# Where the moving operands of a fused attention and two-layer MLP kernel start, modulo 128 bytes

## The chip, the cores and the metric

One core of a Trainium2 chip. The metric is the device time of one execution in microseconds (us), median of the runs; lower is better.

## The reference, cut to what matters

Windowed attention over 4 x 8 heads of 576 positions (head size 64), then two dense layers without bias over 2304 tokens, 512 wide with 2048 hidden units: `relu(h)^2` in the first, `h * cos(h)` in the second. Everything is float32.

```python
def _attn_ref(q, k, v):                       # (4, 8, 576, 64)
    scores = np.matmul(q, k.transpose(0, 1, 3, 2)) / np.sqrt(D)
    rel = pos[:, None] - pos[None, :]
    scores = np.where((rel >= 0) & (rel < 64), scores, -1e9)
    attn = softmax(scores)
    return np.matmul(attn, v)

def reference(**kwargs):
    x = attn_out.transpose(0, 2, 1, 3).reshape(2304, 512)
    h = np.maximum(x @ moe_w_in, 0.0)         # 512 -> 2048
    x = h * h @ moe_w_out                     # 2048 -> 512
    h = x @ moe2_w_in
    return (h * np.cos(h)) @ moe2_w_out
```

## The kernel before

**Products in two words.** A float32 number is held as two words of the type float32r, hi and lo, and each 128x128 block of a product is three matmuls: hi x hi, hi x lo, lo x hi. A matmul reads two operands from the on-chip memory (SBUF): the stationary one, 128 columns, which a weight load puts into TensorE beforehand, and the moving one, 256, 384 or 512 columns that stream past it. A column is 4 bytes in each partition. The weight load for the next matmul runs while the present one streams.

**Stages.** (1) Attention for the first tokens, while the weights of layer 1 are converted. (2) Layer 1 for tokens 0 to 1279 in units (class `UnitA`, and `Half` for the first unit's first four hidden blocks, split in two): `g1` (L1803) multiplies a weight tile `W_in_w...` by the tokens in the tile `X` into `ph`; ScalarE and VectorE make `relu^2` and its hi and lo words in `g`; `g2` (L1129, L1196) multiplies `W` by `g` into `accA`. `g1` of a unit's hidden block runs two blocks ahead of its `g2`, so the two alternate, 12 matmuls each. The attention of later tokens is strewn in. (3) Layer 1 for the last 1024 tokens by Strassen's seven products (`group1`, L1642): the pieces B11, B21, T3 and T4 are in `X`, T1 in a tile `x_more`, T2 and B22 in tiles of their own (`piece`). Its second half is `job1` (L1720, `accC`). (4) Layer 2 in three passes of 768 tokens (`group`, L1514, outputs `x`, `y`, `z`): the 14 pieces of 384 columns lie in `X` and four of them in `x_more` (function `piece`). Its second half is `Job.tile_op` (L1472, `accB`), where the activations `gb_e`, `gb_a`, `gb_b` are stationary and the weights `wo` move.

**What sets the order.** A planner (class `Plan`) orders all operations by keys, due times and modelled costs, and writes them out; the engines then run their queues in order. No address enters the planner.

**Addresses.** Tiles of the pool `cp` stand one after the other at the start of SBUF, and the pools with the weights and activations follow. `X` is laid out as `[P, 2, 2, 4, 512]`. Units 0 and 3 and units 5 and 6 start at column 0 of its halves; unit 2 (256 columns) starts at column 8 of the second (`x_col`). Layer 2's pieces start `SIDE` = 8 columns behind the start of a half. The tiles `g` are 512 columns, read from column 8 where the unit is 256 wide.

Of the kernel before, what the change touches and what calls it, by code (L numbers as in the profile page):

```python
# [9 lines left out]
F32 = mybir.dt.float32  # L10
# [6 lines left out]
P = 128  # L17
# [11 lines left out]
def f32(ap):  # L29
    return ap.bitcast(F32)  # L30
# [212 lines left out]
def kernel(  # L243
# [26 lines left out]
    UA = 256  # L270
    H = 384
    TW = 2 * H
    H1 = 512
# [6 lines left out]
    SIDE = 8  # L280

    psum = bass.MemoryType.PSUM
    cp = ctx.enter_context(tc.tile_pool(name="cp", bufs=1))
# [20 lines left out]
    pair = cp.tile([P, 8], F32, name="hpi")  # L304
    hpi, spare = pair[:, 0:1], pair[:, 4:5]
    quarter = cp.tile([P, 1], F32, name="quarter")
    X = cp.tile([P, 2, 2, NCC, 2 * UA], F32R, name="X")
    still = cp.tile([P, 2, P], F32, name="still")
    nc.vector.memset(still[:, 0], 0.0)
    nc.vector.memset(still[:, 1], 1.0)  # L310
# [14 lines left out]
    def copy(e, o, i, scale=1.0):  # L325
        if e == "ACT":
            nc.scalar.activation(o, i, AF.Copy, scale=scale)  # L327
        elif e == "POOL":
            nc.gpsimd.tensor_scalar(o, i, scale, 1.0, ALU.mult, ALU.mult)
        elif scale == 1.0:  # L330
            nc.vector.tensor_copy(o, i)
        else:
            nc.vector.tensor_scalar(o, i, scale, None, ALU.mult)
# [333 lines left out]


    spans = [(0, 2), (2, 1), (3, 2)]
    x_col = [0, UA, 2 * UA + 8, 0, UA, 2 * UA, 3 * UA]  # L670
    x_before = [
        [m for m in range(n) if abs(x_col[m] - x_col[n]) < UA][-1:] for n in range(len(x_col))]
    xr = R["W"].buf()
# [4 lines left out]
    def packed(n, g, key, sp, k_s=None):  # L678
# [65 lines left out]
        def gather(eng, e):  # L744
# [8 lines left out]
            for i in range(HB):  # L753
# [7 lines left out]
            nc.vector.tensor_reduce(  # L761
                t["mm"][:, e], S[:, :, :, 0:WINDOW], mybir.AxisListType.X, ALU.max, negate=True)

# [98 lines left out]
        def sl(i):  # L862
            return slice(off + i * P, off + i * P + P)

        def hi(eng):
            for i in range(HB):
                copy(eng, X[:, half, 0, cs, sl(i)], t["O"][i])

        def lo(eng):
            for i in range(HB):  # L870
                nc.vector.tensor_tensor(  # L871
                    X[:, half, 1, cs, sl(i)], t["O"][i], f32(X[:, half, 0, cs, sl(i)]), ALU.subtract)

# [8 lines left out]
    def attention(n, g, key, sp, k_s=None):  # L882
# [162 lines left out]
        def hi(eng):  # L1045
            copy(eng, X[:, half, 0, cs, sl], t["O"])

        def lo(eng):
            nc.vector.tensor_tensor(
                X[:, half, 1, cs, sl], t["O"], f32(X[:, half, 0, cs, sl]), ALU.subtract)  # L1050

# [8 lines left out]
    bp = {}  # L1060
# [4 lines left out]
    class UnitA:  # L1065
# [10 lines left out]
        def x(self, hl, c):  # L1076
            return X[:, self.half, hl, c, self.sl]

# [193 lines left out]
    def piece1(o, c, hl):  # L1272
        if o in (B11, B21):
            return X[:, 1, hl, c + 2 * (o == B21)]
        if o in (T3, T4):
            v = X[:, 0].rearrange("p l c n -> p (l c n)")[:, 4 * H1 * (o == T4):][:, 0:4 * H1]
        elif o == T1:
            v = bp["x"][:, SIDE:SIDE + 4 * H1]
        else:
            v = whole1[o].tile  # L1280
        return v[:, (2 * c + hl) * H1:(2 * c + hl + 1) * H1]

    def prepare1(key, free):
# [12 lines left out]
        def whole(o, c):  # L1296
            return f32(piece1(o, c, 0)), f32(piece1(o, c, 1))
# [17 lines left out]
        def split(o, c, src, deps, bufs):  # L1315
            dst = [whole1[o]] if o in whole1 else []

            def hi(e):
                if dst and dst[0].tile is None:
                    dst[0].tile = wp.tile([P, 8 * P * 2], F32R, tag=f"W{dst[0].slot}", name=f"piece_{o}")  # L1320
                copy(e, piece1(o, c, 0), src())

            def lo(e):
                tt(piece1(o, c, 1), src(), f32(piece1(o, c, 0)), ALU.subtract)

            take, used = use(*dst, *bufs)
            h = op({"ACT": act_us(H1), "DVE": dve_us(H1, True)}, key, hi,
                   [*deps, *free.get(o, ())], take, used)
            l = op({"DVE": dve_us(H1)}, key, lo, [h], use=[*dst, *bufs])
            ready1[o, c] = [h, l]  # L1330
            return [h, l]
# [771 lines left out]
```

## Time and profile before

| | |
|---|---|
| median of 3 runs | 837.73 us (836.99 to 841.36) |
| the profiled execution's own time | 836.86 us |
| its span, first to last instruction | 835.1 us |
| matmuls (PE) busy | 827.4 us, 99% of the span |
| weight loads (PEld) busy | 723.8 us |
| VectorE (DVE), ScalarE (ACT) busy | 657.3 us, 470.9 us |

PE is TensorE's matmul side, PEld its weight loads, which run beside matmuls. Matmuls are pipelined: one begins streaming before the one before it has left the array, so that the recorded length of a matmul is more than the distance to the next one's start. This distance is what a matmul costs in a dense stream. It is read from the timeline, where the start of a row less that of the row before it, divided by the number of matmuls in the row before, gives it; rows are given to 0.01 us.

### The profile page before, as it was taken

The page shows a single profiled execution, that of the slowest core. Times are in us where ns is not written, and L with a number is a line of the kernel's source. Part 1 is how long each engine was busy: PE and PEld are TensorE (multiplying, and loading weights), DVE is VectorE, ACT ScalarE, POOL GpSimd, SP SyncE. Part 2 cuts the span into 40 slices and gives each one's busy share as a digit, 9 for nine tenths or more (in the row PEclk, how much of TensorE's full clock was granted, in tenths as well). Part 3 has the DMA queues.
Part 4 walks back from the last instruction along what each step waited for, and adds up shares of the span by engine and source line. Part 5 has one row for each costly group of instructions (what it writes and reads, how often), then busy time and mean ns, then how long its engine had stood idle before and what let it go on. Part 6 is the DMA issues. An engine that isn't in the chain of part 4 may idle for free.

```text
span 835.1 us, 14747 instructions
## 1 busy us (share of the span) xinstructions
PE 827.4 (99%) x5628; PEld 723.8 (87%) x5628; DVE 657.3 (79%) x1325; ACT 470.9 (56%) x1044; POOL 14.4 (2%) x40
## 2 busy tenths in 40 slices
PE   8999999999999999999999999999999999999997
PEld 8898889997787888888888999988999988999986
DVE  6998869889697886776879788885788885788851
ACT  7999546665355743444531656563556653656642
POOL 2300000000000000000000000000000000000000
PEclk9999999999999999999999999999999999999999
DMA  9884157868587749988999693062643062742011
GB/s 346 326 331 139 56 174 277 302 208 312 193 285 273 284 170 370 326 300 312 355 411 375 256 421 117 1 236 105 251 162 104 1 249 92 255 170 93 1 38 38
DMA packets 39797, 181.95 MB, mean 218 GB/s; under 512 B 4016, under 2 KB 6576, under 8 KB 27440
## 3 DMA queue, kind: packets, MB, share of 16 engines
q1 hardware_dynamic: 39728, 181.03, 58.6%
q8 instruction: 44, 0.72, 0.4%
q14 instruction: 25, 0.20, 0.1%
HBM read 129.63 MB, written 51.38 MB: 217 GB/s over the span
## 4 chain that ended last, share of the span: by engine, by line
PE 93%; DVE 4%; ACT 2%; issue 1%; ACTq 0%
PE accB L1472 24%; PE ph L1803 13%; PE accA L1129 12%; PE x L1514 12%; PE accC L1720 9%; PE z L1514 6%; PE x L1642 5%; PE y L1514 3%; PE z L1642 3%; PE O L810 2%; PE S L735 2%; PE y L1642 1%; PE accA L1196 1%; ACT pb L976 1%; PE T L791 1%
## 5 line engine op out<-in xcount | busy, mean ns | idle before, releaser
L1803 PE MATMUL ph<-X,W_in_w_dram 128*128 128x512 f32 (+1 forms) x624 | 124.4, 344 | 0.3 <-DVE X L871 0.3
L1129 PE MATMUL accA<-g,W_in_w_dram 128*128 128x512 f32 (+1 forms) x528 | 110.9, 354 | 0.0
L1803 PEld LDWEIGHTS ph<-X,W_in_w_dram 128*128 128x128 f32 x624 | 98.4, 188 | 14.5 <-DVE X L871 0.5
L1472 PE MATMUL accB<-wo,gb_e 128*128 128x512 f32 x432 | 99.9, 389 | 0.0
L1129 PEld LDWEIGHTS accA<-g,W_in_w_dram 128*128 128x128 f32 x528 | 85.7, 188 | 14.8 <-issue 2.2
L1472 PEld LDWEIGHTS accB<-wo,gb_e 128*128 128x128 f32 x432 | 81.0, 188 | 16.4
L1472 PE MATMUL accB<-wo,gb_b 128*128 128x512 f32 x216 | 53.7, 390 | 0.0
L1472 PE MATMUL accB<-wo,gb_a 128*128 128x512 f32 x216 | 53.4, 389 | 0.0
L373 ACT ACTIVATE raw_in_w_dram<-raw_in_w_dram 128x1024 f32<-128x1024 f32 x32 | 36.7, 1145 | 24.4 <-DMA raw_in_w_dram<-in_w_dram 14.6
L1472 PEld LDWEIGHTS accB<-wo,gb_b 128*128 128x128 f32 x216 | 40.3, 188 | 7.1
L1514 PE MATMUL x<-X,wb 128*128 128x384 f32 x216 | 46.0, 339 | 0.2 <-ACT held L1530 0.2
L1514 PE MATMUL x<-X,wa 128*128 128x384 f32 x216 | 46.0, 339 | 0.0
L1472 PEld LDWEIGHTS accB<-wo,gb_a 128*128 128x128 f32 x216 | 40.2, 188 | 6.6
L1530 ACT ACTIVATE held<-x 128x384 f32<-128x384 f32 x72 | 34.3, 481 | 19.1 <-PE x L1514 19.1
L1720 PE MATMUL accC<-g_k,W_in_w_dram 128*128 128x512 f32 x192 | 44.2, 389 | 0.0
L1720 PEld LDWEIGHTS accC<-g_k,W_in_w_dram 128*128 128x128 f32 x192 | 36.0, 188 | 7.3
L1446 DVE TENSOR_TENSOR gb_e<-keep,gb_e 128x384 fp32r<-128x384 f32 x48 | 26.0, 555 | 20.3 <-ACT gb_e L327 20.2
L1514 PEld LDWEIGHTS x<-X,wa 128*128 128x128 f32 x216 | 39.0, 188 | 2.1
L1093 ACT ACTIVATE r<-ph 128x512 f32<-128x512 f32 (+1 forms) x52 | 26.1, 502 | 23.8 <-PE ph L1803 23.8
L1514 PEld LDWEIGHTS x<-X,wb 128*128 128x128 f32 x216 | 38.5, 188 | 0.7 <-ACT held L1530 0.5
L771 ACT ACTIVATE pb<-S,mm 128x64 f32<-128x64 f32 x112 | 33.4, 325 | 7.0 <-DVE mm L768 7.0
L327 ACT ACTIVATE gb_e<-keep 128x384 fp32r<-128x384 f32 x48 | 24.1, 516 | 22.5 <-PE accB L1472 22.5
(219 smaller groups left out, 1691.1 us busy)
## 6 DMA issues: line engine op xcount, KB each, us to landing
raw_in_w_dram<-in_w_dram SPq DMA_DIRECT2D x32, 1024.0 KB, 8.1
wa<-w2a_dram SPq DMA_DIRECT2D x24, 1024.0 KB, 8.1
wb<-w2b_dram SPq DMA_DIRECT2D x24, 768.0 KB, 7.0
qk<-in_qk_dram SPq DMA_DIRECT2D x17, 576.0 KB, 5.4
v<-in_v_dram SPq DMA_DIRECT2D x18, 512.0 KB, 4.6
w1s_dram<-s SPq DMA_DIRECT2D x8, 1024.0 KB, 4.9
w2a_dram<-w2a SPq DMA_DIRECT2D x8, 1024.0 KB, 5.7
w2o_dram<-w2o SPq DMA_DIRECT2D x8, 1024.0 KB, 8.0
```

Of the source, the lines that this page charges most:

```text
L327: nc.scalar.activation(o, i, AF.Copy, scale=scale)
L373: nc.scalar.activation(hw, hw, AF.Prelu, scale=2.0**-112, alpha=-(2.0**32))
L771: nc.scalar.activation(t["pb"][:, e, r, i], t["S"][e][:, r, i, 0:WINDOW], AF.Exp, bias=t["mm"][:, e, r, i:i + 1], scale=SCALE, accum_out=t ...
L1093: nc.scalar.activation(t["r"], ph()[:, 0:w], AF.Relu)
L1129: nc.tensor.matmul(self.acc[i][:, k, :], w[:, j % 2, wl, m * P:m * P + P], t["g"][:, gl, :], start=(j == 0 and p == 0 and k == 0 and self. ...
L1446: nc.vector.tensor_tensor(t["g"][:, 1], r(), f32(t["g"][:, 0]), ALU.subtract)
L1472: nc.tensor.matmul(acc[0], t["g"][:, gl, m * P:m * P + P], wb.tile[:, k % 2, wl], start=(k == 0 and i == 0), stop=(k == NJ - 1 and i == 2))
L1514: nc.tensor.matmul(ps[x], wb.tile[:, i, wl, c * P:c * P + P], piece(o, c, xl), start=(first and c == 0 and k == 0), stop=(last and c == 1 ...
L1530: return b, op({"ACT": act_us(H)}, key - 6, lambda e: nc.scalar.activation(r_at(b), ps[x], AF.Copy), [dep, o_rooms], [b], [buf], lat=0.39)
L1642: nc.tensor.matmul(ps[x], wb.tile[:, i, wl, c * P:c * P + P] if src is pb or i > 1 else wb.tile[:, wl, i, c * P:c * P + P], piece1(o, c, x ...
L1720: nc.tensor.matmul(acc[0][:, 0], wb.tile[:, k % 2, wl, m * P:m * P + P], t["g"][:, gl, :], start=(k == 0 and p == 0), stop=(k == NJ - 1 an ...
L1803: nc.tensor.matmul(t["ph"][:, 0:u.w], wb.tile[:, j % 2, wl, c * P:c * P + P], u.x(xl, c), start=(c == 0 and k == 0), stop=(c == NCC - 1 an ...
```

## The change

Two unused tiles of 64 bytes are put on either side of `X`, so that `X` alone moves by 64 bytes modulo 128, and all behind it by 128. Unit 2's column in `X` is raised by 16 columns (64 bytes), and so is the start of T1 in `x_more`.

```diff
@@ -304,7 +304,9 @@
     quarter = cp.tile([P, 1], F32, name="quarter")
+    cp.tile([P, 16], F32, name="before")
     X = cp.tile([P, 2, 2, NCC, 2 * UA], F32R, name="X")
+    cp.tile([P, 16], F32, name="behind")
     still = cp.tile([P, 2, P], F32, name="still")
@@ -667,7 +669,7 @@
     spans = [(0, 2), (2, 1), (3, 2)]
-    x_col = [0, UA, 2 * UA + 8, 0, UA, 2 * UA, 3 * UA]
+    x_col = [0, UA, 2 * UA + 24, 0, UA, 2 * UA, 3 * UA]
@@ -1275,7 +1277,7 @@
         elif o == T1:
-            v = bp["x"][:, SIDE:SIDE + 4 * H1]
+            v = bp["x"][:, 3 * SIDE:3 * SIDE + 4 * H1]
```

In the programs as built, every stationary operand of these products starts at byte 64 of 128, before and after. The moving operands start as follows ("ahead" is the moving operand's byte less the stationary one's, modulo 128):

| matmuls | moving operand | columns | number | ahead before | ahead after |
|---|---|---|---|---|---|
| L1803, unit 0 in halves | X | 256 | 96 | 0 | 64 |
| L1803, unit 2 | X | 256 | 192 | 32 | 32 |
| L1803, units 0 and 3 | X | 512 | 336 | 0 | 64 |
| L1642 | X | 512 | 192 | 0 | 64 |
| L1642 | x_more (T1) | 512 | 48 | 0 | 64 |
| L1642 | piece (T2, B22) | 512 | 96 | 0 | 0 |
| L1129, L1196 | g | 256 | 288 | 32 | 32 |
| L1129, L1720 | g | 512 | 720 | 0 | 0 |
| L1514 | X | 384 | 720 | 32 | 96 |
| L1514 | x_more | 384 | 288 | 96 | 96 |
| L1472 | wo | 512 | 864 | 0 | 0 |

Instructions, their order on each engine, their waits and all transfers are the same in both programs; line numbers behind L306 rise by two.

## Rows read from the trace of the kernel before

**Rows 1.** The page: the span, and the chain that ended last by engine.

```profile
span 835.1 us, 14747 instructions
...
PE 93%; DVE 4%; ACT 2%; issue 1%; ACTq 0%
```

**Rows 2.** Waits of PE, longest first: total us, times, longest us.

```profile
PE S L315 <- DVE still L310: 1.3, 1, 1.3
...
PE x L1514 <- ACT held L1530: 0.2, 1, 0.2
```

**Rows 3.** Windows: stretch, length, PE, PEld, DVE, ACT, POOL busy, clock, DMA.

```profile
24.00:305.00 281.00, 280.10 (x2812) 239.62 (x2811) 239.78 (x457) 184.97 (x494) 7.29 (x13) 1.00 0.65 233
305.00:450.00 145.00, 145.00 (x640) 119.72 (x640) 109.00 (x179) 60.12 (x91) 0.00 (x0) 1.00 0.94 352
450.00:830.00 380.00, 379.84 (x1900) 344.32 (x1898) 291.12 (x618) 206.96 (x404) 0.00 (x0) 1.00 0.40 149
```

**Rows 4.** Timeline of PE, layer 2: start us, length us, line, names, count.

```profile
582.01 1.20 PE L1514 MATMUL z<-x_more,wa 128*128 128x384 f32 x6
583.05 1.52 PE L1472 MATMUL accB<-wo,gb_e 128*128 128x512 f32 x6
584.41 0.69 PE L1514 MATMUL x<-x_more,wb 128*128 128x384 f32 x3
...
585.47 1.22 PE L1514 MATMUL x<-X,wa 128*128 128x384 f32 x6
...
589.71 1.54 PE L1472 MATMUL accB<-wo,gb_e 128*128 128x512 f32 x6
```

**Rows 5.** Timeline of PE, one of layer 2's long runs and its neighbours.

```profile
595.22 0.69 PE L1514 MATMUL x<-x_more,wb 128*128 128x384 f32 x3
595.74 0.69 PE L1514 MATMUL x<-X,wb 128*128 128x384 f32 x3
...
600.51 2.22 PE L1472 MATMUL accB<-wo,gb_b 128*128 128x512 f32 x9
602.57 0.69 PE L1514 MATMUL x<-X,wa 128*128 128x384 f32 x3
```

**Rows 6.** Groups by line and shape: count, busy us, mean ns of one.

```profile
L1514 PE MATMUL z<-X,wb 128*128 128x384 f32 x144 | 29.3, 339 | 0.0
L1514 PE MATMUL z<-x_more,wa 128*128 128x384 f32 x144 | 28.9, 336 | 0.0
```

**Rows 7.** Timeline of PE, layer 1: 512 columns, both streams at 0 ahead.

```profile
70.92 2.88 PE L1803 MATMUL ph<-X,W_in_w_dram 128*128 128x512 f32 x12
73.64 2.88 PE L1129 MATMUL accA<-g,W_in_w_dram 128*128 128x512 f32 x12
```

**Rows 8.** The same: 256 columns, X at 0 and g at 32 in turn.

```profile
43.15 1.60 PE L1803 MATMUL ph<-X,W_in_w_dram 128*128 128x256 f32 x12
44.59 1.58 PE L1196 MATMUL accA<-g,W_in_w_dram 128*128 128x256 f32 x12
46.01 1.60 PE L1803 MATMUL ph<-X,W_in_w_dram 128*128 128x256 f32 x12
```

**Rows 9.** The same: unit 2, 256 columns, X and g both at 32.

```profile
145.40 1.56 PE L1803 MATMUL ph<-X,W_in_w_dram 128*128 128x256 f32 x12
...
151.00 1.22 PE L1803 MATMUL ph<-X,W_in_w_dram 128*128 128x256 f32 x9
```

**Rows 10.** The same: 512 columns at 0 between runs of 256 at 32.

```profile
51.71 2.92 PE L1803 MATMUL ph<-X,W_in_w_dram 128*128 128x512 f32 x12
54.47 1.56 PE L1196 MATMUL accA<-g,W_in_w_dram 128*128 128x256 f32 x12
55.87 2.91 PE L1803 MATMUL ph<-X,W_in_w_dram 128*128 128x512 f32 x12
58.61 1.56 PE L1196 MATMUL accA<-g,W_in_w_dram 128*128 128x256 f32 x12
```

**Rows 11.** Timeline of PE: fillers at 0 ahead, and transposes at 64 ahead.

```profile
23.62 0.61 PE L315 MATMUL ph<-still 128*128 128x128 f32 x4
...
98.13 0.60 PE L791 MATMUL T<-ident,pb 128*128 128x128 f32 x4
```

**Rows 12.** Groups by line and shape: count, busy us, mean ns of one.

```profile
L315 PE MATMUL ph<-still 128*128 128x128 f32 x4 | 0.6, 275 | 0.0
L791 PE MATMUL T<-ident,pb 128*128 128x128 f32 x56 | 8.4, 273 | 0.1
```

## The prediction

> **What bounds the kernel now.** I read the chain that ended last first: PE holds 93% of it [rows 1]. The list of waits then says whether PE ever stands still: the longest single wait is 1.3 us at the very start, and in layer 2 there is one of 0.2 us [rows 2]. The table by stage closes the question: in the three stages that hold the products PE is busy for 280.10 of 281, 145.00 of 145 and 379.84 of 380 us, at a granted clock of 1.00, which is the 2.4 GHz level [rows 3]. So the time is a sum of distances between the starts of matmuls, and a nanosecond off each of a thousand is a microsecond off the end. No transfer and no other engine has to be moved for that: VectorE, the next busiest, has 291.12 us of work in layer 2's 380 [rows 3], so a few microseconds less there leave it ahead.
>
> The change alters nothing but addresses, so the only thing to price is how the distance between matmuls depends on where the moving operand starts relative to the stationary one. The trace of before holds three of the four positions in steps of 32 bytes: 0, 32 and 96 ahead. 64 ahead, where layer 1 goes, is not there for these products.
>
> **Layer 2, 720 matmuls from 32 to 96.** The same product, the same shape and the same weights run from `X` at 32 and from `x_more` at 96. Six matmuls from `x_more` take 583.05 - 582.01 = 1.04 us, 173.3 ns each; 24 from `X` take 589.71 - 585.47 = 4.24 us, 176.7 ns each [rows 4]. The recorded length says the same from another column: 339 ns against 336 [rows 6]. That these 3.3 ns come from the position and not from the tile is likely, since the position is the sole thing in which the two reads differ, and since one tile, `X`, shows two distances in layer 1 at two positions (below). So: 720 x 3.3 ns = 2.4 us less.
>
> Edges come on top. After a run that ends on `X`, nine `accB` matmuls take 602.57 - 600.51 = 2.06 us [rows 5]; six after a run that ends on `x_more` take 584.41 - 583.05 = 1.36 us, 226.7 each [rows 4], and nine at that rate would take 2.04. So a run that ends on `X` leaves 0.02 us to the `accB` behind it, and 30 of layer 2's 54 runs end so: up to 0.6 us more. Against it, the first matmuls from `x_more` after `accB` are not free either: three take 0.52 us [rows 5], which the rounding lets be 0.01 above 3 x 173.3; over 54 runs up to 0.5 us. I take +0.2 us of gain for both edges together, and layer 2 as **-2.6 us**, between 0 (if the position is not the cause) and -3.0.
>
> **Layer 1, 576 matmuls of 512 columns and 96 of 256, from 0 to 64.** At 0, 12 matmuls of 512 take 73.64 - 70.92 = 2.72 us, 226.7 ns each [rows 7]. 128 columns more cost 226.7 - 173.3 = 53.4 ns, 0.417 each, one clock of 2.4 GHz; 512 of them are 213.3 ns, so 13.3 ns of each matmul is something else. The 384-column ones have 173.3 - 160 = 13.3 ns of it at 96 and 16.7 at 32. With 256 columns, `X` at 0 between runs of `g` at 32 takes (44.59 - 43.15) / 12 = 120 ns, and `g` at 32 then (46.01 - 44.59) / 12 = 118.3 [rows 8]; where both stand at 32, 48 matmuls take 5.60 us, 116.7 ns each [rows 9]. So a position is worth 3.3 ns of a matmul in both comparisons, and 0 has the 13.3 ns that the better position has at 384 columns. 64 is not measured: by the nearest rows it may be 3.3 ns better or 3.3 ns worse than 0, which over 672 matmuls is -2.2 to +2.2 us. The row nearest in shape is 512 columns at 0 itself, and it shows no more of the extra than the best of 384. I take no change, **0.0 us**, and keep both ends.
>
> Switching has a price of its own. Twelve matmuls of 512 at 0 take 2.72 us among their like, but 54.47 - 51.71 = 2.76 and 58.61 - 55.87 = 2.74 us next to runs at 32 [rows 10]: 0.02 to 0.04 us a run. Now all of layer 1's 512-column work stands at 0; afterwards runs at 64 and at 0 alternate, 42 times from 64 to 0 and back. 42 x 0.02 = 0.8 us if the switch costs what it costs from 32, nothing if it is like the one from `x_more` at 96 to `accB` at 0, which left 226.7 ns. I take **+0.4 us**.
>
> The rule of the Trainium skill that bears on this speaks against the change: its page "SBUF — State Buffer", section "SBUF: two separate sides", says that on the engine side only the port pair shared by VectorE and GpSimd causes contention, and that PE never waits on anyone; "TensorE: Matmul & The Clock Gate", section "Step-by-step: what each phase is for", gives PE two independent read ports, one for each operand. By it every term above is zero. The trace disagrees, with 176.7 against 173.3 ns at one shape.
>
> **Sum.** -2.6 + 0.0 + 0.4 = -2.2 us. The profiled execution took 836.86 us, 0.87 below the median of the runs shown, 837.73; off the median that is **835.5 us**. A measurement of this kernel tells some 0.5% (4.2 us) from no change, so the forecast is a small gain that counts as the same.
>
> **The rivals.**
> *64 is a better place for the wide ones too* (chance 0.22). If it is worth the same 3.3 ns as the two other comparisons, layer 1 gives -2.2 us: -2.6 - 2.2 + 0.4 = -4.4, 833.3 us, right at the bound. For it: both moves that the trace shows, 32 to 96 and 0 to 32, gained as much. Against it: 0 is already at the lower level.
> *64 takes the two reads out of each other's way altogether* (0.08). The transposes have their operands 64 apart, and four take 0.60 us with 273 ns for the last, so (600 - 273) / 3 = 109 ns each, 2.3 above the 106.7 of two clocks a column; the fillers at 0 need (610 - 275) / 3 = 111.7 [rows 11, 12]. If the extra of 13.3 ns fell to 2 here as well: 576 x 11.3 = 6.5 us, with at most 96 x 11 = 1.0 us from the narrow ones: -2.6 - 7.5 + 0.4 = -9.7, 828.0 us. Against it: a transpose moves 128 columns in 109 ns, half as many a nanosecond as the products, and the fillers at 0 lie close to it.
> *64 is a worse place, and the switching spoils its neighbours* (0.2). 226.7 ns may be a rhythm that only a stream at one position keeps; next to runs at 32 the same matmuls came to 2.76 / 12 = 230 ns [rows 10]. If the 576 went to 230, layer 1 gives +1.9, the narrow ones +0.3 and switching +0.8, together +3.0: 838.1 us. It is slower than before from a loss in layer 1 of 2.6 us on, 4.5 ns a matmul, and by more than 0.5% only from 6.8 us on, 11.8 ns, which no row here shows: one in five of this rival at most. If the 720 matmuls of `g` at 0 are dragged along, 1296 x 4.3 ns = 5.6 us: 840.7 us.
> *Position does nothing* (0.08), and `X` against `x_more` has another cause: 837.7 us. For it stands the rule above by itself; against it stands that `X` has two distances at 256 columns.
> The forecast itself, 834.2 to 836.7 us, has 0.42.
>
> **Range and chances.** The forecast, the no-effect case, most of the worse case and the near part of the better one lie between 831.0 and 839.0 us; outside are the altogether free case (0.08), the far part of the worse one (0.05) and a little of the better one (0.03). Faster by over 0.5% are the free case and half of the better one, 0.19; slower by over 0.5% the end of the worse one, 0.04; the same 0.77.
>
> **What would show it.** In layer 2 the matmuls from `X` should stand 173.3 ns apart, with a recorded length of 336 rather than 339, and `accB` behind every run at 226.7 from its second matmul on; 176.7 would refute the main term. In layer 1 the decisive number is twelve `ph` from `X` in the stretch where no attention stands between: 2.72 us is my forecast, 2.68 the better case, 2.60 or less the free one, 2.76 the worse one; and the twelve `accA` from `g` that follow tell the price of switching: 2.72 none, 2.74 and more what I fear. Should PE wait more in layer 2 than 0.2 us, the gain has turned into idle time. The step most likely to be wrong is the position 64, which nothing in this trace has.

## The result, and the profile after

The changed kernel takes 843.32 us, median of 7 runs (842.45 to 843.93); the kernel before, on the same chip, 837.57 us (7 runs, 836.99 to 841.36). The ratio over the runs is 1.0063 [1.0051, 1.0075] (the quotient of the two medians is 1.0069): slower by more than the 0.5% that the prediction set as its bound, and 4.3 us above the upper end of its range. The profiled execution took 842.48 us.

The page of the changed kernel: the span, busy time by engine, and the chain that ended last by engine.

```profile
span 840.8 us, 14747 instructions
...
PE 832.6 (99%) x5628; PEld 722.1 (86%) x5628; DVE 657.3 (78%) x1325; ACT 469.9 (56%) x1044; POOL 14.3 (2%) x40
...
PE 93%; DVE 3%; ACT 2%; DMA 1%; issue 1%; SPq 0%; ACTq 0%
```

The windows of the same three stages [rows 3], columns as there.

```profile
24.00:305.00 281.00, 280.50 (x2808) 238.13 (x2807) 238.84 (x454) 184.03 (x493) 7.21 (x13) 1.00 0.64 232
305.00:450.00 145.00, 145.00 (x634) 118.63 (x633) 107.63 (x177) 60.87 (x92) 0.00 (x0) 1.00 0.92 346
450.00:830.00 380.00, 379.81 (x1888) 341.32 (x1887) 293.86 (x624) 205.17 (x402) 0.00 (x0) 1.00 0.40 151
```

PE is as busy as before, at the same granted clock of 1.00, and it gets through fewer matmuls in the same time: 2808, 634 and 1888 where before had 2812, 640 and 1900 [rows 3]. The span grew by 5.7 us, PE's busy time by 5.2. So no new wait holds the kernel up; the matmuls themselves stand further apart. The waits of PE, columns as in [rows 2], say the same: the longest is new, but it is 1.7 us, at an attention load where before had 0.5.

```profile
PE S L955 <- DMA qk<-in_qk_dram: 1.7, 1, 1.7
...
PE x L1516 <- ACT held L1532: 0.2, 1, 0.2
```

Timeline of PE in layer 1, for [rows 7].

```profile
71.24 2.96 PE L1805 MATMUL ph<-X,W_in_w_dram 128*128 128x512 f32 x12
74.04 2.90 PE L1131 MATMUL accA<-g,W_in_w_dram 128*128 128x512 f32 x12
76.78 2.96 PE L1805 MATMUL ph<-X,W_in_w_dram 128*128 128x512 f32 x12
```

Twelve `ph` take 74.04 - 71.24 = 2.80 us, 233.3 ns each, where they took 226.7; the twelve `accA` behind them, whose operands did not move against each other, take 76.78 - 74.04 = 2.74 where they took 2.72.

Timeline of PE in layer 2, for [rows 4].

```profile
585.68 1.22 PE L1516 MATMUL z<-x_more,wa 128*128 128x384 f32 x6
586.74 1.56 PE L1474 MATMUL accB<-wo,gb_e 128*128 128x512 f32 x6
588.14 0.69 PE L1516 MATMUL x<-x_more,wb 128*128 128x384 f32 x3
...
589.20 1.21 PE L1516 MATMUL x<-X,wa 128*128 128x384 f32 x6
...
593.36 1.54 PE L1474 MATMUL accB<-wo,gb_e 128*128 128x512 f32 x6
```

The 24 from `X` now take 593.36 - 589.20 = 4.16 us, 173.3 ns each, as forecast. But six from `x_more`, which nobody touched, take 1.06 us, 176.7 each instead of 173.3, and six `accB` take 1.40 us, 233.3 instead of 226.7.

**Where the positions really are.** The front part counts "ahead" modulo 128. Modulo 256 the programs as built differ in more than that table shows. Weights, `wo`, `g`, `gb_a` and half of `gb_e` lie behind `X` on the left side of the memory and were pushed by the 128 bytes of the two pads; `x_more`, `gb_b` and the other half of `gb_e` lie in a pool on the right side and stayed. The mean distances below are worked out from the starts of all matmuls of a kind in the two traces that have a matmul close behind them.

| matmuls | ahead mod 256, before | ns | after | ns | number x difference, us |
|---|---|---|---|---|---|
| layer 1, X, 512 columns | 0 | 227.8 | 192 | 233.2 | 528: +2.8 |
| layer 1, T1 | 0 | 226.7 | 192 | 233.3 | 48: +0.3 |
| layer 1, g and T2, B22, 512 columns | 0 | 227.6 | 0 | 228.3 | 816: +0.6 |
| layer 1, X, unit 0 in halves | 0 | 119.4 | 192 | 115.1 | 96: -0.4 |
| layer 2, X | 32 | 176.7 | 224 | 174.2 | 720: -1.8 |
| layer 2, x_more | 224 | 174.2 | 96 | 176.6 | 288: +0.7 |
| `accB`, gb_a and half of gb_e | 0 | 226.9 | 0 | 230.3 | 432: +1.5 |
| `accB`, gb_b and half of gb_e | 0 | 227.5 | 128 | 233.1 | 432: +2.4 |

They add up to +6.1 us, where PE's busy time grew by 5.2 and the span by 5.7; the 0.9 us more than PE's busy time shows is not placed. The two lines of `accB`, which the front's table gives as unchanged, are the largest item.

### The profile page after: what moved, and what is told of

Read it like the earlier page. It is cut to its first block, busy times and chain, and to the rows that moved or that the text cites. A ratio compares the mean times of both kernels' runs of the same rounds, so it can differ in the third digit from the quotient of the medians.

```text
span 840.8 us, 14747 instructions
## 1 busy us (share of the span) xinstructions
PE 832.6 (99%) x5628; PEld 722.1 (86%) x5628; DVE 657.3 (78%) x1325; ACT 469.9 (56%) x1044; POOL 14.3 (2%) x40
## 4 chain that ended last, share of the span: by engine, by line
PE 93%; DVE 3%; ACT 2%; DMA 1%; issue 1%; SPq 0%; ACTq 0%
PE accB L1474 24%; PE ph L1805 13%; PE accA L1131 12%; PE x L1516 12%; PE accC L1722 8%; PE z L1516 6%; PE x L1644 5%; PE y L1516 3%; PE z L1644 3%; PE O L812 2%; PE S L737 2%; PE y L1644 1%; PE accA L1198 1%; DMA qk<-in_qk_dram 1%; PE T L793 1%; ACT pb L978 1%
## 5 line engine op out<-in xcount | busy, mean ns | idle before, releaser
L1474 PE MATMUL accB<-wo,gb_e 128*128 128x512 f32 x432 | 102.0, 394 | 0.0
```

The costliest lines, as they stand in the source:

```text
L1474: nc.tensor.matmul(acc[0], t["g"][:, gl, m * P:m * P + P], wb.tile[:, k % 2, wl], start=(k == 0 and i == 0), stop=(k == NJ - 1 and i == 2))
```

## The experiments

Two theories were put against each other. A: the distance goes by the difference of the two start bytes modulo 256, and the pads changed it for `x_more` and `accB` because these read one operand from either side of the memory. B: it goes modulo 128, and the changed layer 1, or the products from `X` at their new place, put the streams behind them out of step. Ratios are taken over all runs, against the kernel before, whose median beside them was 837.59 to 838.23 us.

**128 bytes in front of X, and nothing else.**

```diff
+    cp.tile([P, 32], F32, name="before")
     X = cp.tile([P, 2, 2, NCC, 2 * UA], F32R, name="X")
```

> The kernel before with one unused tile of 128 bytes in front of X: modulo 128 every operand stands as before, modulo 256 what lies on the left side of SBUF (X, W, wo, g, gb_a, half of gb_e) is moved against what lies on the right (x_more, gb_b, the other half of gb_e). Theory A (the positions count modulo 256, and the change moved left against right by 128): accB about 231.5 ns instead of 227.2 (863 x 4.4 = +3.8 us), x_more in layer 2 176.6 instead of 174.2 (+0.7 us), sum +4 to +5 us, some 842 us. Theory B (the positions count modulo 128, and accB is slower in the changed kernel because the products in front of it stand at 96 and leave it out of step): no change, 837.6 us, accB 227.2 ns.

Measured: 840.1 us, ratio 1.0031 [1.002, 1.0042], span 837.9. Timeline of PE in layer 2:

```profile
583.17 1.22 PE L1515 MATMUL z<-x_more,wa 128*128 128x384 f32 x6
584.24 1.57 PE L1473 MATMUL accB<-wo,gb_e 128*128 128x512 f32 x6
585.64 0.69 PE L1515 MATMUL x<-x_more,wb 128*128 128x384 f32 x3
...
586.69 1.20 PE L1515 MATMUL x<-X,wa 128*128 128x384 f32 x6
...
590.85 1.55 PE L1473 MATMUL accB<-wo,gb_e 128*128 128x512 f32 x6
```

Modulo 128 nothing has changed, and yet six from `x_more` take 1.07 us and six `accB` 1.40, as in the changed kernel. So 128 is no period, and the shift of left against right alone does this. Layer 1's products from `X`, whose two operands the pad pushed together, stay at 227.8 ns in the mean: it is the difference of the two bytes that counts there, and not either byte by itself. One thing came unasked: the 24 from `X`, at 32 as before, take 590.85 - 586.69 = 4.16 us instead of 4.24. That gave back 2.0 us, so the whole came to 2.5 us and not more.

**The change without its pads.** `X` is laid out ahead of the two small tiles `pair` and `quarter`, which puts it 64 bytes lower and leaves everything behind it where it was (all diffs are against the kernel before):

```diff
+    X = cp.tile([P, 2, 2, NCC, 2 * UA], F32R, name="X")
     pair = cp.tile([P, 8], F32, name="hpi")
     ...
-    X = cp.tile([P, 2, 2, NCC, 2 * UA], F32R, name="X")
-    x_col = [0, UA, 2 * UA + 8, 0, UA, 2 * UA, 3 * UA]
+    x_col = [0, UA, 2 * UA + 24, 0, UA, 2 * UA, 3 * UA]
-            v = bp["x"][:, SIDE:SIDE + 4 * H1]
+            v = bp["x"][:, 3 * SIDE:3 * SIDE + 4 * H1]
```

> The changed kernel without its two unused tiles; X is moved by 64 bytes by being laid out in front of two small tiles instead. X stands to W exactly as in the changed kernel (192 and 224 modulo 256), left stands to right as in the kernel before. Theory A: layer 2 gains what was forecast (x from X 174.2, x_more 174.2, accB 227.2 ns), layer 1 keeps its loss (233.3 ns, 576 matmuls, about +3 us), sum 838 to 839.5 us. Theory B: as the changed kernel, 843.3 us, accB 231.7 ns.

Measured: 838.37 us, ratio 1.0013 [1.0003, 1.0023], span 836.7. Timeline of PE in layer 2:

```profile
585.21 1.20 PE L1514 MATMUL z<-x_more,wa 128*128 128x384 f32 x6
586.25 1.52 PE L1472 MATMUL accB<-wo,gb_e 128*128 128x512 f32 x6
587.61 0.69 PE L1514 MATMUL x<-x_more,wb 128*128 128x384 f32 x3
...
588.66 1.20 PE L1514 MATMUL x<-X,wa 128*128 128x384 f32 x6
...
592.82 1.52 PE L1472 MATMUL accB<-wo,gb_e 128*128 128x512 f32 x6
```

`x_more` is back at 1.04 us, `accB` at 1.36, and `X` keeps its 4.16. Timeline of PE in layer 1:

```profile
71.67 2.96 PE L1803 MATMUL ph<-X,W_in_w_dram 128*128 128x512 f32 x12
74.47 2.90 PE L1129 MATMUL accA<-g,W_in_w_dram 128*128 128x512 f32 x12
```

The loss from `X` in layer 1 is still whole: twelve `ph` at 192 take 2.80 us, 233.3 ns each. Only T1 is not where the changed kernel has it: without the pads it stands at 64, and takes 231.7 ns. Theory A holds and B falls.

**Layer 2's pieces in X at 96, and at 224.** One number in `piece`, the rest as before (56 in place of 24 for the second kernel):

```diff
-        return X[:, half].rearrange("p l c n -> p (l c n)")[:, SIDE + k * H:SIDE + k * H + H]
+        return X[:, half].rearrange("p l c n -> p (l c n)")[:, 24 + k * H:24 + k * H + H]
```

> The kernel before with layer 2's pieces in X alone moved by 64 bytes (16 columns): 96 ahead modulo 128 and modulo 256; layer 1 and all tiles stand as before. Theory A: 96 is not 224, where x_more stood: X stays at about 176.6 ns, no gain, 837 to 838 us. Theory B: X at 173.5 to 174.2 ns, -2 us or more unless accB gets out of step (then +2 us).

> The kernel before with layer 2's pieces in X alone moved by 192 bytes (48 columns): 224 ahead modulo 256, as x_more stands; 96 modulo 128 as in the run before this one. Theory A: X at 174.2 ns, accB 227.2 ns, -2 to -2.6 us, 835.3 us. Theory B: the same as the run with 96.

At 96: 838.12 us, ratio 1.0008 [0.9996, 1.002]. At 224: 835.47 us (835.06 to 836.0, 8 runs), ratio 0.9971 [0.996, 0.9981], span 833.9. Timelines of PE in layer 2, at 96 first:

```profile
586.18 1.22 PE L1514 MATMUL x<-X,wa 128*128 128x384 f32 x6
...
590.42 1.54 PE L1472 MATMUL accB<-wo,gb_e 128*128 128x512 f32 x6
```

```profile
585.94 1.20 PE L1514 MATMUL x<-X,wa 128*128 128x384 f32 x6
...
590.10 1.52 PE L1472 MATMUL accB<-wo,gb_e 128*128 128x512 f32 x6
591.46 0.69 PE L1514 MATMUL x<-X,wa 128*128 128x384 f32 x3
```

At 96 the 24 take 4.24 us, 176.7 ns each, no better than at 32; at 224 they take 4.16, and `accB` behind them 1.36. So what the prediction read off `x_more` was the price of 224, not of 96. This one number, without pads, beats both kernels.

**A map of the positions by itself.** This kernel computes no part of the reference. For 512, 384 and 256 columns it runs 36 matmuls in a row at each of the sixteen positions in steps of 32 bytes, each behind twelve at 0. It ran once, and the granted clock is 1.00 while the matmuls run:

```python
for i in range(k):
    nc.tensor.matmul(t[:, 0:n], W[:, (0, 0, 1, 2, 2, 3)[i % 6]], X[:, base // 4:base // 4 + n], ...)
```

> No part of the reference is computed: only matmuls of 512, 384 and 256 columns in the order hi, hi, lo of the weights, 36 in a row with the moving operand 0, 32, ..., 480 bytes ahead of the stationary one, each row behind 12 at 0. Theory A (period 256 bytes): the second half of the list repeats the first. 512 columns: 226.7 ns at 0 and 233.3 at 192, 64 and 128 at about 232; 384 columns: 173.3 at 224, some 176.7 at 32 and 96; 256 columns: 116.7 at 32, 114 at 192. Theory B (period 128 bytes): 0 equals 128 and 32 equals 160; 224 equals 96.

Mean distance in ns, the start of the next row less a row's own, by 36:

| columns | 0 | 32 | 64 | 96 | 128 | 160 | 192 | 224 |
|---|---|---|---|---|---|---|---|---|
| 512 | 226.7 | 233.3 | 229.4 | 233.6 | 233.1 | 233.9 | 233.3 | 233.6 |
| 384 | 173.3 | 173.3 | 173.1 | 176.4 | 176.1 | 176.7 | 173.1 | 173.6 |
| 256 | 120.0 | 117.8 | 117.8 | 120.0 | 118.6 | 117.5 | 113.9 | 118.3 |

The column of 0 is from the position 256. The positions 288 to 480 repeat 32 to 224 within 0.3 ns in all three shapes (the last row of all has none behind it and is left out). Some of the timeline's rows (the tile's name gives columns and position):

```profile
27.11 8.42 PE L35 MATMUL w512at64x<-X,W 128*128 128x512 f32 x36
35.37 2.93 PE L35 MATMUL w512zero<-X,W 128*128 128x512 f32 x12
...
71.60 8.56 PE L35 MATMUL w512at192x<-X,W 128*128 128x512 f32 x36
80.00 2.90 PE L35 MATMUL w512zero<-X,W 128*128 128x512 f32 x12
...
93.89 8.32 PE L35 MATMUL w512at256x<-X,W 128*128 128x512 f32 x36
102.05 2.88 PE L35 MATMUL w512zero<-X,W 128*128 128x512 f32 x12
...
160.42 8.56 PE L35 MATMUL w512at448x<-X,W 128*128 128x512 f32 x36
168.82 2.90 PE L35 MATMUL w512zero<-X,W 128*128 128x512 f32 x12
```

36 at 192 take 80.00 - 71.60 = 8.40 us, 36 at 448 = 192 + 256 take 8.40 too, 36 at 256 take 8.16, and 36 at 64 take 8.26. The period is 256 bytes; 512 columns have one good place, 0; 384 columns have three bad ones, 96 to 160; 256 columns have one that is better than the rest, 192. What stands at the foot of all this is not shown by any run: which part of the engine or of its reads makes the extra.

**What the map promises: all of layer 2 at 0, unit 2 at 192, both together.** By the map 0 is good for 384 columns, and 192 for 256.

```diff
-            return bp["x"][:, (i - 10) * H:(i - 9) * H]
+            return bp["x"][:, SIDE + (i - 10) * H:SIDE + (i - 9) * H]
-        return X[:, half].rearrange("p l c n -> p (l c n)")[:, SIDE + k * H:SIDE + k * H + H]
+        return X[:, half].rearrange("p l c n -> p (l c n)")[:, k * H:k * H + H]
```

```diff
-    x_col = [0, UA, 2 * UA + 8, 0, UA, 2 * UA, 3 * UA]
+    x_col = [0, UA, 2 * UA + 48, 0, UA, 2 * UA, 3 * UA]
-            at = 8 if w == UA else 0
+            at = 48 if w == UA else 0
```

> The kernel before with all of layer 2's pieces, in X and in x_more, at 0 ahead modulo 256, as accB stands. By the map: 173.3 ns for 384 columns, and no switch between positions, so no loss at the 108 borders of runs: 720 x 3.3 + 288 x 0.8 ns + 0.3 us at accB = -2.9 us, 834.7 us. Were 0 good for 512 columns alone, or the borders not due to the position: as the run with 224, -2.1 us.

> The kernel before with unit 2's columns in X and every 256-column g at 192 ahead instead of 32. By the map 113.9 instead of 117.9 ns for 256 columns, where both streams stand there (unit 2, 384 matmuls less the first few of each run after attention): -1.0 us, 836.5 us. If 192 loses what it gains at the switches to 0 (first unit's halves) and to attention: no change.

> Both of the two edits before this one together: their sum, -3.5 to -4 us, 833.6 to 834.2 us, if each acts on its own stage; less if not.

Measured: layer 2 at 0, 838.31 us, ratio 0.9996 [0.9984, 1.0009]; unit 2 at 192, 837.24, 0.9997 [0.9981, 1.0012]; both, 838.93, 1.001 [0.9992, 1.0027]. None tells itself from no change. Timeline of PE with layer 2 at 0:

```profile
583.66 1.55 PE L1472 MATMUL accB<-wo,gb_e 128*128 128x512 f32 x6
585.05 0.69 PE L1514 MATMUL x<-x_more,wb 128*128 128x384 f32 x3
...
586.09 1.20 PE L1514 MATMUL x<-X,wa 128*128 128x384 f32 x6
...
590.25 1.55 PE L1472 MATMUL accB<-wo,gb_e 128*128 128x512 f32 x6
...
592.69 1.20 PE L1514 MATMUL z<-x_more,wa 128*128 128x384 f32 x6
593.73 2.24 PE L1472 MATMUL accB<-wo,gb_a 128*128 128x512 f32 x9
595.81 0.68 PE L1514 MATMUL x<-x_more,wb 128*128 128x384 f32 x3
```

The products take 4.16 us, as the map says. But six `accB`, at 0 as ever, take 585.05 - 583.66 = 1.39 us where they take 1.36 behind products at 224. Over the whole layer the products from `X` gain 1.7 us (176.7 to 174.3 ns), `accB` loses 1.6 (227.2 to 229.1) and `x_more` 0.3 (174.2 to 175.2). Both streams stand at their good place, and the border between them costs what the products gained: the map's price of a stream holds for a long one, and does not tell what a run of six or nine does behind another shape.

Timeline of PE with unit 2 at 192, for [rows 9]:

```profile
147.81 1.52 PE L1803 MATMUL ph<-X,W_in_w_dram 128*128 128x256 f32 x12
149.17 1.52 PE L1129 MATMUL accA<-g,W_in_w_dram 128*128 128x256 f32 x12
```

Twelve take 1.36 us, 113.3 ns each, against 116.7 in [rows 9]. In the stretches with attention between them they gain less: the means over all of them fall by 1.0 ns for `X` and 1.6 for `g`, some 0.6 us over 480 matmuls, and the span is 0.2 us shorter (834.9 against 835.1). That is below what a timing tells.

**Layer 1's part alone.** `X` ahead of the small tiles as above, layer 2's pieces and unit 2 moved back to 32 inside it, T1 at 0:

```diff
-    x_col = [0, UA, 2 * UA + 8, 0, UA, 2 * UA, 3 * UA]
+    x_col = [0, UA, 2 * UA + 24, 0, UA, 2 * UA, 3 * UA]
-        return X[:, half].rearrange("p l c n -> p (l c n)")[:, SIDE + k * H:SIDE + k * H + H]
+        return X[:, half].rearrange("p l c n -> p (l c n)")[:, 24 + k * H:24 + k * H + H]
```

> The kernel before with layer 1's operands in X alone at 192 ahead modulo 256, where the changed kernel has them (528 of the 576 matmuls of 512 columns; T1 in x_more stays at 0); layer 2 stays at 32 and 224, left stands to right as before. By the difference of the runs with X laid ahead and with layer 2 at 224 (838.37 - 835.47), and by the map (233.3 against 226.7 ns): 528 x some 5.5 ns = +2.9 us, and a few tenths for g behind it, 840.5 us; accB in layer 2 at 227.2 ns. Were the loss of the changed kernel all from left against right: no change.

Measured: 839.73 us, ratio 1.0032 [1.002, 1.0045]; the kernel before took 837.59 beside it, so the loss is 2.1 us in the median, where 2.9 was expected. The span of the profiled execution, 837.8 us, is 2.7 above before. Timeline of PE:

```profile
76.44 2.96 PE L1803 MATMUL ph<-X,W_in_w_dram 128*128 128x512 f32 x12
79.24 2.90 PE L1129 MATMUL accA<-g,W_in_w_dram 128*128 128x512 f32 x12
```

Twelve `ph` take 2.80 us, and `accB` in layer 2 is at its 227 to 228 ns. The loss stays in layer 1.

**The two gains together**: layer 2 at 224 by `56 + k * H`, and unit 2 at 192 as above.

> Layer 2's pieces in X at 224 and the 256-column streams of unit 2 and every narrow g at 192, the two single edits that took time out of their own stage. Sum of the two runs' traces, -2.1 and -0.3 to -0.6 us: 835 us, the same as the run with 224 alone or a little less.

Measured: 835.01 us (833.7 to 838.06, 9 runs), ratio 0.9971 [0.9961, 0.9981], span 833.3. It is the lowest median of all, but its ratio is that of 224 alone; the part of unit 2 does not show in the timing.

## Why the prediction was wrong

- **What bounds the kernel** was right. PE is the sum of its distances before and after, no engine and no transfer took over, and its waits add up to 3.8 us against 3.4.
- **The measure of position was wrong, and this is the step that failed first.** The prediction took "ahead" modulo 128, as the front's table gives it. The map shows a period of 256. With it three statements fall: `x_more` did not stand at 96 but at 224; layer 1 went to 192 and not to 64; and the two pads, together 128 bytes, were not neutral for what lies behind them. The sum has no term for `accB` and none for `x_more`, which came to +3.9 and +0.7 us. The kernel with 128 bytes of padding and nothing else shows that the shift by 128 causes them: its `x_more` takes 176.7 ns and its `accB` 229.8 to 232.1, near those of the changed kernel (176.6, 230.5 to 232.9), and without pads both are back. Of the +3.9, their own position explains the 2.4 us of the half that went to 128; the other half stayed at 0 and is spoken of below. The prediction gave an outcome slower by over 0.5% a chance of 0.04.
- **Layer 2, -2.6 us** from `X`: right in that the start byte sets the distance, and nearly in its size, -1.8 in the changed kernel; by itself, at 224, it takes 2.1 us off the median. The reason given (96 is better than 32) was wrong: at 96 itself there is nothing to be had. That 173.3 ns came out is luck: the pads moved the weights by 128 and `X` by 64, which put it at 224, where `x_more` had been read. The charge for edges was set too high: it counted 54 runs that begin with `x_more`, and 24 do.
- **Layer 1, 0.0 us between -2.2 and +2.2**: mis-sized. It is 6.7 ns a matmul from a steady 226.7, twice the bound, and +3.1 us by the means over the 576; the part alone costs 2.7 in the span. Part of this is the wrong measure again, since the place is 192 and not 64: at 64 the map has 229.4 ns, within the bound, though T1 took 231.7 there. The bound of 3.3 ns came from 384 and 256 columns. The map shows that 512 columns have a scale of their own: 6.7 ns lie between 0 and nearly all other places, and 384 columns know only half of that. The remark that 0 already had the lower level at 512 was the right one, and should have spoken for a loss.
- **Switching, +0.4 us**: right in its size, though the switch is from 192 and not from 64. Twelve `accA` behind `ph` take 2.74, the value that the prediction named for it, and by the means it comes to +0.6.
- **The rivals.** "64 is a worse place" ended on the right side, but with 230 ns a matmul where 233.3 came, and at 838.1 us; the layer 1 part alone took 839.73. Its other half, neighbours dragged along, came true in `accB` rather than in `g`, and from the pads rather than from switching. "Position does nothing" is refuted: at one shape and a granted clock of 1.00 the map has 226.7 and 233.9 ns. The Trainium skill's page "TensorE: Matmul & The Clock Gate" (section "Step-by-step: what each phase is for") gives the engine two independent read ports; whether the extra arises at them no run here shows.

Why `accB` with `gb_a`, at 0 in both kernels, goes from 227.0 to 230.5 ns in the changed one is known in part. Neither products from `X` at 224 nor at 96 do it by themselves (226.9 and 227.1 ns), and `accB` at 128 is not needed for it: with layer 2 at 0, where no `accB` stands there, `gb_a` takes 230.7. Eighteen of its runs, nine matmuls each, stand directly behind products from `x_more`; one of them in the kernel before:

```profile
603.62 1.20 PE L1514 MATMUL z<-x_more,wa 128*128 128x384 f32 x6
604.66 2.20 PE L1472 MATMUL accB<-wo,gb_a 128*128 128x512 f32 x9
606.71 0.52 PE L1514 MATMUL x<-x_more,wb 128*128 128x384 f32 x2
```

These nine take 2.05 us, and 2.08 in the rows shown for layer 2 at 0. Over all eighteen the mean is 226.9 ns with `x_more` at 224 (before, and with `X` at 96 or 224), 231.2 with it at 0, and with it at 96 it is 231.0 in the changed kernel and 229.4 behind the pad of 128 bytes. So the extra goes with the place of the products just ahead. `x_more` alone was not moved, and why the place ahead matters is not shown. The weights' own byte was not tried apart from the difference, but it did change: the programs as built have it at 192 of 256 in the kernel before, at 64 behind the pad of 128 bytes and at 128 in the map, and 512 columns at 0 from `X` ran at 226.7 ns in dense stretches of all three. Shapes other than these three were not tried.

## What to carry to other kernels

Where the matmuls stand densely, compute for each stream the start of the moving operand less that of the stationary one, from the program as built and with more digits than the pattern you expect, and hold it against distances read between starts; here the period was 256 bytes, and a table modulo 128 hid the largest term. A pad moves all that lies behind it on its side of the memory against all on the other side, so shift a view inside its tile (one number in an index, here 2.1 us for nothing) rather than the tile. Measure a new position by a row of long streams first, and then once more in place, since a border between two streams can cost what the place gives.

## What the runs showed of the hardware that was not expected

- The distance between float32r matmuls repeats with 256 bytes of difference between the two start bytes: 226.7 ns at 0 and 229.4 to 234.2 elsewhere for 512 columns, 173.1 to 173.6 or 176.1 to 176.7 for 384, 113.6 to 120.0 for 256. The best place depends on the width: 0 alone for 512, 192 alone for 256, and five places alike for 384 (0, 32, 64, 192, 224).
- One position can have two rhythms: 384 columns at 32 took 176.7 ns in the kernel before, and 173.3 in the map and behind the pad of 128 bytes. The weights' own byte differed too (192 of 256 in the kernel before, 128 in the map, 64 behind the pad); whether this picks the one or the other is open.
- What runs just ahead of a short run changes its distance: behind products at 0, six `accB` at 0 took 1.39 us; behind products at 224, 1.36.
